# Four PSUM banks held for good in one tile, and an earlier start of two dense tiles

## The chip, the cores and the metric

The kernel runs on one core of one Trainium2 chip. The metric is device time in microseconds (us), the median of several executions. All runs used below were marked as fast ones, and each kernel's ratio is taken against runs of the kernel before on the same chip. Differences between two other kernels are of medians, some from different chips; the kernel before took 335.0 to 335.7 us on all of them.

## The reference

The reference computes an attention over eight batches of eight heads, 576 tokens and 64 values per head: a pooled attention on every fourth position plus a local one over a narrow band. The result becomes `x` with 4608 rows of 512, and goes through two dense layers. Cut to what matters here:

```python
def reference(q, k, v, moe_w_in, moe_w_out):
    attn_out = _attn_ref(q, k, v)                 # [8, 8, 576, 64]; pooled + banded
    x = attn_out.transpose(0, 2, 1, 3).reshape(4608, 512)
    h = x @ moe_w_in                              # 512 -> 2048
    g = h - np.tanh(h)
    return g @ moe_w_out                          # 2048 -> 512
```

## The kernel before

The kernel does not issue its instructions by hand. Each step is declared with its engine, an estimated cost, and the keys that it reads and writes; a list scheduler written in the kernel's own Python fixes one order of all steps, and the instructions are built in that order. The framework that builds the program then adds the semaphore waits, from the tiles that each instruction touches. So there are two systems of dependencies: the scheduler's keys decide the order, and the framework's tiles decide what waits for what.

The kernel uses eight banks of PSUM, where TensorE leaves its results. Four (`ps_ts`, `ps_ox`) serve attention throughout. The other four first serve the attention of batch 0 as two tiles of two banks, and then the dense layers as four tiles of one bank:

```python
ps_ts = fixed("ps_ts", [128, 2, 512], FP32, pool=psum)
ps_ox = fixed("ps_ox", [128, 2, 512], FP32, pool=psum)
ps_hy = []

early = ExitStack()
psum_e = early.enter_context(tc.tile_pool(name="psum_e", bufs=1, space=PSUM))
ps_ts1 = fixed("ps_ts1", [128, 2, 512], FP32, pool=psum_e)
ps_ox1 = fixed("ps_ox1", [128, 2, 512], FP32, pool=psum_e)

def dense_banks():
    early.close()
    pool = ctx.enter_context(tc.tile_pool(name="psum_d", bufs=1, space=PSUM))
    ps_hy.extend(fixed("ps_hy", [128, 512], FP32, 4, pool=pool))
```

One tile of the first dense layer is four matmuls (K chunks 0 to 3, one per pair of heads), a tanh on ScalarE and a subtract on VectorE, both reading the bank:

```python
def mm1(kb, fc):
    slot, us, g = hy[0] % 4, un[0] % 3, kb % 2
    # ... cut
    cut = 3 if kb == 0 and fc < 4 else 2
    old = ["ts1", "ox1"] if kb == 0 and fc < 4 else []

    def mm(part):
        if not ps_hy:
            dense_banks()
        for dc in range(cut) if part == 0 else range(cut, N_DC):
            T.matmul(ps_hy[slot], w_in_sb[:, dc, fc * 128:(fc + 1) * 128],   # L777
                     xT[dc][:, kb * 512:kb * 512 + 512],
                     start=(dc == 0), stop=(dc == N_DC - 1))
    # ... the two parts become two steps on PE, of keys ("hy", slot) and old
    op("ACT", 490, lambda: A.activation(                                     # L786
        out=u[us], in_=ps_hy[slot], func=AF.Tanh), ...)
    op("DVE", 620, lambda: V.tensor_tensor(                                  # L789
        out=gT[g][:, fc, :], in0=ps_hy[slot], in1=u[us], op=ALU.subtract), ...)
```

The second dense layer (`mm2`) adds up 16 matmuls (L832) into one bank, which ScalarE copies out (L843). The scheduler interleaves them: usually two to four matmuls of one layer, then of the other, on different banks. One "round" below is the work for one output tile: 32 matmuls, four tanh, four subtracts and one copy. There are 36 of them.

The softmax here doesn't subtract the row's maximum and nothing guards it: scores larger than these inputs give would overflow.

## Time and profile before

| | before |
|---|---|
| time, median (range) | 334.98 us (334.89 to 335.55) |
| profiled span | 333.9 us |
| mean granted TensorE clock | 1.000 |
| TensorE idle | 333.9 - 319.9 = 14.0 us (rather less: 43 of 2606 matmuls left no record) |
| last attention matmul, then dense work only | one round takes 6.9 us |

The prediction shows the busy shares, groups and timelines that the argument rests on. One more row of the page belongs with them, the granted clock: the span is cut into 40 slices, and each digit is the clock that TensorE was granted in that slice, in tenths (9 is 90% or more).

```profile
PEclk9999999999999999999999999999999999999999
```

The clock is full from end to end.

### The profile page before, as it was taken

The page shows a single profiled execution, that of the slowest core. Times are in us where ns is not written, and L with a number is a line of the kernel's source. Part 1 is how long each engine was busy: PE and PEld are TensorE (multiplying, and loading weights), DVE is VectorE, ACT ScalarE, POOL GpSimd, SP SyncE. Part 2 cuts the span into 40 slices and gives each one's busy share as a digit, 9 for nine tenths or more (in the row PEclk, how much of TensorE's full clock was granted, in tenths as well). Part 3 has the DMA queues.
Part 4 walks back from the last instruction along what each step waited for, and adds up shares of the span by engine and source line. Part 5 has one row for each costly group of instructions (what it writes and reads, how often), then busy time and mean ns, then how long its engine had stood idle before and what let it go on. Part 6 is the DMA issues. An engine that isn't in the chain of part 4 may idle for free.

```text
span 333.9 us, 6822 instructions
## 1 busy us (share of the span) xinstructions
PE 319.9 (96%) x2563; PEld 168.2 (50%) x2606; DVE 236.0 (71%) x386; ACT 209.6 (63%) x338; POOL 154.2 (46%) x183
## 2 busy tenths in 40 slices
PE   8778999999989999999999999999999999999996
PEld 5454555655554555554444444444444444444444
DVE  3697989789998898899687878787666443343300
ACT  1775877769948678668878786976654444444411
POOL 8673766248789477794929385652000000000000
PEclk9999999999999999999999999999999999999999
DMA  6999999999982779998999889843233000100012
GB/s 208 261 389 305 322 326 287 242 273 251 311 258 72 214 191 273 242 248 221 226 257 253 210 239 204 152 97 90 59 75 73 33 31 31 63 33 31 31 69 91
DMA packets 96878, 60.47 MB, mean 181 GB/s; under 512 B 74510, under 2 KB 80078, under 8 KB 96846
## 3 DMA queue, kind: packets, MB, share of 16 engines
q1 hardware_dynamic: 96846, 60.04, 67.2%
q8 instruction: 20, 0.33, 0.4%
q14 instruction: 12, 0.10, 0.1%
HBM read 43.05 MB, written 9.44 MB: 157 GB/s over the span
## 4 chain that ended last, share of the span: by engine, by line
PE 83%; DVE 9%; POOL 3%; issue 3%; ACT 1%; POOLq 0%; DVEq 0%; ACTq 0%
PE ps_hy L832 35%; PE ps_hy L777 34%; PE ps_ox L669 3%; PE ps_ts L587 3%; PE ps_ox L675 2%; DVE gT L789 2%; DVE ln L688 2%; PE ps_ts L520 2%; PE ps_hy L807 1%; DVE E L656 1%; DVE qk L529 1%; DVE half L533 1%; ACT qk L529 1%; DVE E L627 1%; PE ps_ox L606 1%
## 5 line engine op out<-in xcount | busy, mean ns | idle before, releaser
L777 PE MATMUL ps_hy<-xT,w_in_sb 128*128 128x512 bf16 x553 | 142.1, 379 | 2.3 <-issue 1.1
L832 PE MATMUL ps_hy<-w_out_sb,gT 128*128 128x512 bf16 x540 | 137.2, 379 | 1.4 <-issue 0.5
L789 DVE TENSOR_TENSOR gT<-ps_hy,uy 128x512 bf16<-128x512 f32 x144 | 95.1, 684 | 57.9 <-ACT uy L786 56.3
L786 ACT ACTIVATE uy<-ps_hy 128x512 f32<-128x512 f32 x144 | 83.6, 601 | 61.7 <-PE ps_hy L777 57.2
L777 PEld LDWEIGHTS <-w_in_sb 128*128 128x128 bf16 x576 | 53.1, 98 | 59.8 <-issue 1.7
L832 PEld LDWEIGHTS <-gT 128*128 128x128 bf16 x560 | 52.3, 98 | 58.1
L533 POOL TENSOR_TENSOR half<-qk 128x576 f32<-128x576 bf16 (+1 forms) x33 | 35.4, 1074 | 44.2 <-ACT qk L529 38.2
L688 DVE TENSOR_TENSOR ln<-ps_ox,r 128x896 bf16<-128x896 f32 x30 | 32.7, 1089 | 0.8
L623 ACT ACTIVATE E<-ps_ts 128x960 bf16<-128x960 f32 x30 | 29.4, 979 | 2.1 <-PE ps_ts L587 2.1
L843 ACT COPY uy<-ps_hy 128x512 f32<-128x512 f32 x35 | 20.6, 590 | 14.0 <-PE ps_hy L832 12.4
L443 POOL CAST vw<-vst 128x640 bf16<-128x640 f32 x27 | 23.6, 878 | 9.3 <-DMA vst<-in_v_dram 4.3
L627 DVE TENSOR_TENSOR E<-E,mask 128x960 bf16<-128x960 bf16 x28 | 24.4, 872 | 4.0 <-ACT E L623 3.8
L356 POOL TENSOR_TENSOR qkn<-qkn 128x512 f32<-128x512 f32 (+1 forms) x18 | 25.4, 1409 | 3.1 <-PE ps_ox L606 1.3
L529 ACT COPY qk<-ps_ts 128x1152 bf16<-128x1152 bf16 (+1 forms) x16 | 16.1, 1007 | 16.2 <-DVE qk L529 6.3
L708 DVE TENSOR_TENSOR xT<-lnT 128x480 bf16<-128x480 bf16 (+1 forms) x40 | 26.1, 668 | 0.0
L529 ACT COPY qk<-vst 128x1152 bf16<-128x1152 bf16 x10 | 22.1, 2207 | 1.2 <-POOL half L533 1.2
L538 POOL TENSOR_TENSOR qkd<-half 128x288 bf16<-128x288 f32 (+1 forms) x31 | 20.5, 664 | 5.0 <-DVE half L533 3.7
L491 DVE CAST qr<-qkn 128x1152 bf16<-128x1152 f32 (+1 forms) x18 | 17.8, 987 | 2.6 <-DMA qkn<-in_q_dram 2.2
L669 PEld LDWEIGHTS <-E 128*128 128x128 bf16 x300 | 15.2, 98 | 7.2 <-issue 0.8
L587 PEld LDWEIGHTS <-qk 64*128 64x128 bf16 x320 | 9.5, 95 | 17.8 <-issue 15.6
L669 PE MATMUL ps_ox<-vw,E 128*128 128x65 bf16 x300 | 18.0, 194 | 0.3 <-DVE xT L734 0.3
L491 POOL CAST qr<-qkn 128x1152 bf16<-128x1152 f32 (+1 forms) x14 | 15.8, 1129 | 5.1 <-DMA qkn<-in_k_dram 3.0
(107 smaller groups left out, 295.8 us busy)
## 6 DMA issues: line engine op xcount, KB each, us to landing
vst<-in_v_dram SPq DMA_DIRECT2D x62, 160.0 KB, 5.0
qkn<-in_q_dram SPq DMA_DIRECT2D x32, 288.0 KB, 4.2
qkn<-in_k_dram SPq DMA_DIRECT2D x32, 288.0 KB, 5.0
out_dram<-uy SPq DMA_DIRECT2D x35, 256.0 KB, 2.4
qkn<-in_v_dram SPq DMA_DIRECT2D x9, 512.0 KB, 5.1
gT<-in_moe_w_in_dram SPq DMA_DIRECT2D x4, 1024.0 KB, 8.8
xT<-in_moe_w_out_dram SPq DMA_DIRECT2D x8, 256.0 KB, 4.9
gT<-in_moe_w_out_dram SPq DMA_DIRECT2D x2, 1024.0 KB, 9.0
```

Source lines behind the costliest of these rows:

```text
L491: P.choice([(eng, ns, lambda fn=fn, x0=x0, x1=x1: fn(out=dst[:, x0:x1], in_=srt[:, x0:x1])) for eng, ns, fn in table], reads=[("qkn", sn, ...
L529: fn(out=o[:, ys].rearrange("p y (g a) -> p y g a", a=A6), in_=b16.rearrange("p (a g y) -> p y g a", a=A6, y=2)[:, ys])
L533: eng.tensor_tensor(out=half[:, ys], in0=four[:, ys, :, 0:2], in1=four[:, ys, :, 2:4], op=ALU.add)
L623: op("ACT", 980, lambda: A.activation(out=e1, in_=ps[:, :, 0:480], func=AF.Exp, scale=SCALE), reads=ts, writes=[("E", se, 0)], pri=URG.get ...
L627: op("DVE", 900, lambda: V.tensor_tensor(out=e1, in0=e1, in1=mask[:, 0:480].unsqueeze(1).to_broadcast([128, 2, 480]), op=ALU.mult), reads= ...
L669: T.matmul(po[:, hh, 65 * t:65 * t + 65], E[se][:, c:c + 128], vw[w][:, 2 * jj + hh, t, :], start=True, stop=True)
L688: op("DVE", 1090, lambda: V.tensor_tensor(out=ln[sl].rearrange("p n (h d) -> p h n d", d=D), in0=blocks[:, :, :, 0:64], in1=r[s].unsqueeze ...
L708: up=up: eng.tensor_tensor(out=xo[:, QW * t0:QW * t0 + nt * n].rearrange("p (t g a) -> p t g a", t=nt, a=4), in0=lnT[sl][:, t0:t0 + nt, 0: ...
L777: T.matmul(ps_hy[slot], w_in_sb[:, dc, fc * 128:(fc + 1) * 128], xT[dc][:, kb * 512:kb * 512 + 512], start=(dc == 0), stop=(dc == N_DC - 1))
L786: op("ACT", 490, lambda: A.activation(out=u[us], in_=ps_hy[slot], func=AF.Tanh), reads=[("hy", slot)], writes=[("u", us)], pri=-1)
L789: op("DVE", 620, lambda: V.tensor_tensor(out=gT[g][:, fc, :], in0=ps_hy[slot], in1=u[us], op=ALU.subtract), reads=[("hy", slot), ("u", us) ...
L832: T.matmul(ps_hy[slot], gT[g][:, fc, ts * 128:ts * 128 + 128], w_out_sb[:, fc, :], start=(fc == 0), stop=(fc == N_FF - 1))
```

## The change

The intent is to save the closing and opening of pools between batch 0 and the dense layers: the four banks become one tile for good, and both uses are slices of it. With the banks no longer tied to a pool that opens when all of batch 0's use is over, two dense tiles may begin on K chunks 0 and 1 in the two banks that pair 0 leaves first. Tables that say on which engine a copy or an addition goes, and how urgent a step is, were tuned anew.

```diff
-    ps_hy = []
-    early = ExitStack()
-    psum_e = early.enter_context(tc.tile_pool(name="psum_e", bufs=1, space=PSUM))
-    ps_ts1 = fixed("ps_ts1", [128, 2, 512], FP32, pool=psum_e)
-    ps_ox1 = fixed("ps_ox1", [128, 2, 512], FP32, pool=psum_e)
-
-    def dense_banks():
-        early.close()
-        pool = ctx.enter_context(tc.tile_pool(name="psum_d", bufs=1, space=PSUM))
-        ps_hy.extend(fixed("ps_hy", [128, 512], FP32, 4, pool=pool))
+    ps_e = fixed("ps_e", [128, 4, 512], FP32, pool=psum)
+    ps_ts1, ps_ox1 = ps_e[:, 0:2], ps_e[:, 2:4]
+    ps_hy = [ps_e[:, 2], ps_e[:, 3], ps_e[:, 0], ps_e[:, 1]]
 ...
-        cut = 3 if kb == 0 and fc < 4 else 2
-        old = ["ts1", "ox1"] if kb == 0 and fc < 4 else []
+        old, parts = [], (range(0, 2), range(2, 4))
+        if kb == 0 and fc < 4:
+            old = ["ox1"] if fc < 2 else ["ts1"]
+            parts = (range(0, 2), range(2, 3), range(3, 4)) if fc < 2 else (range(3), range(3, 4))
 ... (mm takes the list of chunks; one step on PE per part)
-    P_A, LATE = 5000, {0: 25, 2: 40, 3: 40}
+    P_A, LATE = 5000, {0: 40, 2: 40, 3: 40}
-    PV = {2: 0, 3: 0, 4: -1, 5: -1, 6: 0}
+    PV = {2: 0, 3: 1, 4: -1, 5: 0, 6: 1}
 ... (so too PLACE, CV, RE, TU, PV1, VD, RS, UP, TS, AS, URG and AD: entries of tables)
```

More of the change, by code (lines that the diff above doesn't have):

```diff
@@ L768, in mm1, with mm @@
         bs = sorted({kb * 512 // S, (kb * 512 + 511) // S})
-        cut = 3 if kb == 0 and fc < 4 else 2
-        old = ["ts1", "ox1"] if kb == 0 and fc < 4 else []
-        def mm(part):
-            if not ps_hy:
-                dense_banks()
-            for dc in range(cut) if part == 0 else range(cut, N_DC):
+        old, parts = [], (range(0, 2), range(2, 4))
+        if kb == 0 and fc < 4:
+            old = ["ox1"] if fc < 2 else ["ts1"]
+            parts = (range(0, 2), range(2, 3), range(3, 4)) if fc < 2 else (range(3), range(3, 4))
+        def mm(dcs):
+            for dc in dcs:
                 T.matmul(ps_hy[slot], w_in_sb[:, dc, fc * 128:(fc + 1) * 128],
@@ L779, in mm @@
                          start=(dc == 0), stop=(dc == N_DC - 1))
-        for part in range(2):
-            dcs = range(cut) if part == 0 else range(cut, N_DC)
-            op("PE", 216 * len(dcs), lambda part=part: mm(part),
+        for dcs in parts:
+            op("PE", 216 * len(dcs), lambda dcs=dcs: mm(dcs),
                reads=[("w_in", fc // 4, c) for c in dcs] +
                [(name, b, j) for b in bs for j in dcs for name in ("x", "xh")],
-               writes=[("hy", slot)] + old, pri=P_A if old and part == 0 else 5000)
+               writes=[("hy", slot)] + old, pri=P_A if old and dcs[-1] < 3 else 5000)
         op("ACT", 490, lambda: A.activation(
@@ L881 @@
     TB = {(1, 0), (1, 1), (2, 0), (2, 1), (3, 0), (5, 0)}
-    PV = {2: 0, 3: 0, 4: -1, 5: -1, 6: 0}
-    PLACE = {2: (1, 3), 3: (1, 2), 4: (4, 4), 5: (1, 2), 6: (4, 4), 7: (1, 1), 8: (3, 3)}
+    PV = {2: 0, 3: 1, 4: -1, 5: 0, 6: 1}
+    PLACE = {2: (0, 2), 3: (1, 2), 4: (4, 4), 5: (1, 2), 6: (4, 4), 7: (1, 1), 8: (3, 3)}
     W_LATE = [0, 0, 0, 0]
@@ L890 @@
               [("DVE", 500, V.tensor_copy)]]
-    CV = {0: 3, 1: 0, 2: 0, 3: 3, 4: 0, 5: 0, 6: 3, 7: 1, 8: 2, 9: 0, 10: 1, 11: 3}
+    CV = {0: 3, 1: 1, 2: 1, 3: 3, 4: 1, 5: 0, 6: 3, 7: 0, 8: 2, 9: 0, 10: 2, 11: 3}
     REORDER = [[("DVE", 860, V.tensor_copy), ("ACT", 950, A.copy),
@@ L895 @@
                [("DVE", 1150, V.tensor_copy)], [("POOL", 1350, GP.tensor_copy)]]
-    RE = {(0, 0): 0, (0, 1): 0, (1, 0): 1, (1, 1): 1, (2, 0): 1, (2, 1): 0, (3, 0): 3, (3,
-          1): 0, (4, 0): 2, (4, 1): 1, (5, 0): 0, (5, 1): 0}
+    RE = {(0, 0): 1, (0, 1): 4, (1, 0): 2, (1, 1): 4, (2, 0): 3, (2, 1): 4, (3, 0): 0, (3,
+          1): 0, (4, 0): 2, (4, 1): 4, (5, 0): 1, (5, 1): 1}
     TURN = [[("ACT", 1125, A.copy), ("DVE", 1250, V.tensor_copy)],
@@ L900 @@
             [("ACT", 2210, A.copy)]]
-    TU = {(0, 0): 0, (0, 1): 0, (1, 0): 2, (1, 1): 2, (2, 0): 0, (2, 1): 0, (3, 0): 2, (3,
-          1): 0, (4, 0): 0, (4, 1): 1, (5, 0): 1, (5, 1): 0}
+    TU = {(0, 0): 2, (0, 1): 1, (1, 0): 2, (1, 1): 1, (2, 0): 1, (2, 1): 1, (3, 0): 2, (3,
+          1): 1, (4, 0): 1, (4, 1): 1, (5, 0): 1, (5, 1): 1}
     re_v, re_a, re_p = (("DVE", 480, V.tensor_copy), ("ACT", 580, A.copy),
@@ L908 @@
               [("ACT", 600, A.copy)], [("DVE", 650, V.tensor_copy)]]
-    PV1 = True
-    VD = {0: 1, 1: 2, 2: 1, 3: 0, 4: 1, 5: 0, 6: 1}
-    RS = {(0, 1): 2, (1, 0): 4, (1, 1): 1}
-    UP = {0: 0, 1: 0, 2: 0, 3: 3, 4: 3, 8: 0, 11: 3}
+    PV1 = False
+    VD = {0: 2, 1: 0, 2: 1, 3: 1, 4: 1, 5: 0, 6: 1}
+    RS = {(0, 1): 2, (1, 0): 4, (1, 1): 3, (3, 0): 4}
+    UP = {0: 3, 1: 0, 2: 3, 3: 3, 4: 2, 6: 3, 8: 1, 11: 3}
     UP_COPY = [("ACT", 660, A.copy), ("DVE", 720, V.tensor_copy)]
@@ L920 @@
              [[half_p], [half_p]]]
-    TS = {(0, 0): 1, (0, 1): 2, (1, 1): 2, (2, 1): 2, (4, 0): 2, (5, 0): 2, (5, 1): 1}
-    AS = {(1, 0): 2, (1, 1): 1, (2, 0): 1, (2, 1): 1, (5, 0): 1, (5, 1): 4, (6, 1): 1}
-    URG = {'e1': {4: -2, 5: -2, 6: -2, 7: -2, 8: -2, 9: -2, 10: -2, 11: -2}, 'e2': {0: -2,
-          1: -2, 2: -2, 3: -2, 4: -2, 5: -2, 6: -2, 7: -2, 8: -2, 9: -2, 10: -2, 11: -2},
-          'norm': {0: -2, 1: -2, 2: -2, 3: -2, 4: -2, 5: -2, 6: -2, 7: -2}, 'add': {0: -2,
-          1: -2}, 'turn': {4: -2, 5: -2}, 'vd': {4: -2, 5: -2}}
+    TS = {(0, 0): 1, (0, 1): 2, (1, 1): 2, (2, 1): 2, (5, 0): 1, (5, 1): 3}
+    AS = {(0, 0): 1, (1, 0): 1, (1, 1): 1, (2, 0): 1, (4, 0): 1, (5, 0): 4, (5, 1): 4, (6,
+          1): 1}
+    URG = {'e1': {8: -2, 9: -2, 10: -2, 11: -2}, 'e2': {0: -2, 1: -2, 2: -2, 3: -2, 4: -2,
+          5: -2, 6: -2, 7: -2, 8: -2, 9: -2, 10: -2, 11: -2}, 'od': {0: -2, 1: -2}, 'norm':
+          {0: -2, 1: -2, 2: -2, 3: -2, 4: -2, 5: -2, 6: -2, 7: -2, 8: -2, 9: -2, 10: -2, 11:
+          -2}, 'add': {0: -2, 1: -2, 2: -2, 3: -2, 4: -2, 5: -2, 6: -2, 7: -2}, 'turn': {4:
+          -2, 5: -2}, 'vd': {2: -2, 3: -2}}
     ADDERS = [[("DVE", 760, 440, V), ("POOL", 1190, 850, GP)],
               [("POOL", 1190, 880, GP)], [("DVE", 760, 440, V)]]
-    AD = {(0, 0): 1, (0, 1): 0, (1, 0): 0, (1, 1): 1, (2, 0): 1, (2, 1): 0, (3, 0): 0, (3,
-          1): 1, (4, 0): 0, (4, 1): 0, (5, 0): 0, (5, 1): 2}
+    AD = {(0, 0): 2, (0, 1): 2, (1, 0): 0, (1, 1): 1, (2, 0): 0, (2, 1): 1, (3, 0): 0, (3,
+          1): 1, (4, 0): 0, (4, 1): 0, (5, 0): 2, (5, 1): 1}
     op("DVE", 180, lambda: V.memset(warm, 0.0), writes=["warm"], pri=-999)
```

## The prediction

> **What bounds the kernel now.** I read the page first: busy shares, then the group table, then the chain of waits.
>
> ```profile
> PE 319.9 (96%) x2563; PEld 168.2 (50%) x2606; DVE 236.0 (71%) x386; ACT 209.6 (63%) x338; POOL 154.2 (46%) x183
> PE 83%; DVE 9%; POOL 3%; issue 3%; ACT 1%; POOLq 0%; DVEq 0%; ACTq 0%
> L777 PE MATMUL ps_hy<-xT,w_in_sb 128*128 128x512 bf16 x553 | 142.1, 379 | 2.3 <-issue 1.1
> L832 PE MATMUL ps_hy<-w_out_sb,gT 128*128 128x512 bf16 x540 | 137.2, 379 | 1.4 <-issue 0.5
> L789 DVE TENSOR_TENSOR gT<-ps_hy,uy 128x512 bf16<-128x512 f32 x144 | 95.1, 684 | 57.9 <-ACT uy L786 56.3
> L786 ACT ACTIVATE uy<-ps_hy 128x512 f32<-128x512 f32 x144 | 83.6, 601 | 61.7 <-PE ps_hy L777 57.2
> L843 ACT COPY uy<-ps_hy 128x512 f32<-128x512 f32 x35 | 20.6, 590 | 14.0 <-PE ps_hy L832 12.4
> ```
>
> TensorE carries 83% of the chain, nearly all of it dense matmuls. Its idle column is tiny (2.3 and 1.4 us), while VectorE and ScalarE wait 58 and 62 us for each other and for it: they are followers. The timeline of a late stretch shows why TensorE does not wait for them:
>
> ```profile
> 259.04 1.03 PE L832 MATMUL ps_hy<-w_out_sb,gT 128*128 128x512 bf16 x4
> 259.24 0.60 ACT L786 ACTIVATE uy<-ps_hy 128x512 f32<-128x512 f32 x1 [1.07 <-PE ps_hy L777]
> 259.87 0.69 DVE L789 TENSOR_TENSOR gT<-ps_hy,uy 128x512 bf16<-128x512 f32 x1 [0.87 <-ACT uy L786]
> 259.90 1.03 PE L777 MATMUL ps_hy<-xT,w_in_sb 128*128 128x512 bf16 x4
> 260.77 1.89 PE L832 MATMUL ps_hy<-w_out_sb,gT 128*128 128x512 bf16 x8
> ```
>
> While ScalarE (259.24) and VectorE (259.87) read one finished bank, TensorE fills others. Four matmuls start every 0.86 us, 0.216 us each (eight take 1.89 = 7 x 0.216 + 0.379); a matmul's record of 0.379 is thus 0.216 of its own plus 0.163 of tail.
>
> The change aims at the timeline just before the dense layers:
>
> ```profile
> 28.66 0.81 PE L777 MATMUL ps_hy<-xT,w_in_sb 128*128 128x512 bf16 x2
> ...
> 28.85 0.40 ACT L734 CAST xT<-ps_ts 128x288 bf16<-128x288 f32 x1
> 29.29 0.46 DVE L734 CAST xT<-ps_ts 128x288 bf16<-128x288 f32 x1 [0.54 <-ACT xT L734]
> ...
> 29.80 1.46 PE L777 MATMUL ps_hy<-xT,w_in_sb 128*128 128x512 bf16 x6 [0.33 <-DVE xT L734]
> ```
>
> Dense work begins at 28.66 and then waits for the last K chunk. From 29.80 on, TensorE's waits of 0.2 us or more add up to about 1.3 us (0.30, 0.65 and 0.33 at 53, 94 and 101 us). Note also the two copies in the middle: the two halves of this copy lie in the two different banks of one tile, yet VectorE waited until ScalarE ended (29.25, plus 0.04). Waits in this program go by tile here, not by bank.
>
> **What the Trainium skill says.** "PSUM — Partial Sum Buffer", section "PSUM bank collisions raise a hardware error", says that two engines must not touch the same bank and quadrant at once, but pairs on different banks run clean. The trace agrees at 259 us: three engines at work on ps_hy, no wait. So four dense banks need no ordering among themselves. "TensorE: Matmul & The Clock Gate", section "Back-to-back issue gap", gives N/2.4 + 2.5 ns, 216 ns for 512 columns, as measured here. The same page's "A second HAM failure mode: psum-queue depth-cycling" tells of a kernel whose short idles between groups of matmuls made the clock oscillate; the kernel before never shows it (granted clock 1.00 in every stretch).
>
> **The change part by part.** (1) Two tiles may start on K chunks 0 and 1 early. In the built order only two matmuls move ahead of pair 3's last step, and four more follow it before the last chunk is needed: six done instead of three, so 3 x 0.216 = 0.65 us at best. (2) The tables move copies and adds among ScalarE, VectorE and GpSimd; what TensorE idles after 29.80 caps this at 1.3 us, plus perhaps a microsecond of start. The stated gain is therefore 1 to 3 us of 335, under 1%.
>
> (3) The dense banks were four tiles (ps_hy0 to ps_hy3); now they are slices of one tile, ps_e. I followed the waits of the built program to the instructions that raise the semaphores. In the program before, a tanh waits for its own bank's last matmul, and a bank's next matmul for its own subtract. In the changed one, every change of engine on ps_e is ordered against the access just before it, whichever bank that used: all 588 of 588 such changes, 575 of them between different banks. For instance the third K chunk of tile 1 waits for the tanh of tile 0; that tanh waits for tile 1's second chunk. So TensorE's dense matmuls, the tanh, the subtract and the output copies form one strict chain in which one engine works at a time.
>
> The chain after the first dense matmul has 255 runs of TensorE, 173 of ScalarE and 140 of VectorE. Its sum, from the rows above:
> - Until the first dense matmul, as before: 28.7.
> - TensorE: (576 + 560) x 0.216 = 245.4, and 3.5 for the 48 narrower matmuls of the last tile: 248.9.
> - ScalarE: 144 x 0.601 + 35 x 0.590 = 107.2, and three small copies, 1.0: 108.2.
> - VectorE: 144 x 0.684 = 98.5, and two small copies, 0.7: 99.2.
> - Handovers. From TensorE, 255 x (0.163 tail + 0.04) = 51.8. Into TensorE, 254 x 0.04 = 10.2; between the other two, 58 x 0.04 = 2.3. The 0.04 is what stood between ScalarE's end and VectorE's start at 29.25. In 165 handovers the wait stands on a separate wait instruction; the last two of these lines, from the end of the chain of waits, show 0.08 in place of 0.04:
>
> ```profile
> 327.40 3.55 PE ps_hy L807 x48
> 330.95 0.03 DVEq L815
> 330.99 0.04 issue
> 331.03 0.29 DVE uy L815
> ```
>
>   so 165 x 0.04 = 6.6 more. Together 70.9.
> - Attention matmuls. By their widths some 52 us follow the first dense one; by their place in the order about 34 stand where TensorE waits anyway, and 17.5 inside a run, where they lengthen the chain: 17.5.
> - The end: from 331.3 to 333.9, 2.6; and the timed figure is 1.1 above the profiled span (334.98 against 333.9).
>
> Sum: 28.7 + 248.9 + 108.2 + 99.2 + 70.9 + 17.5 + 2.6 + 1.1 = 577. To this I add what can only be guessed: in 139 places ScalarE or VectorE has attention work (241 us in all) between two steps of the chain. There is room for each in those gaps, but inputs that come late will hold up some tanh or subtract. At 0.12 us a place, my choice, that is 17 us: **594 us**.
>
> **Rivals.** *The chain does not bind, and the stated gain comes:* 332 to 335 us. For it: the hardware needs no such waits, and the copies on ScalarE and VectorE are short. Against it: the waits are in the program, and the halves at 29.29 show one holding an engine back across banks. I give it 2 to 3%. *The chain binds, but attention fills the holes better or worse:* this moves the 17.5 and the 17. If all attention matmuls fall into waits, 560; if each of the 139 places costs 0.5 us, 647. *The clock falls:* TensorE would be at work for about 300 of 594 us in pieces of 0.4 to 2 us with idles of 0.7 to 1.5. If such idles count as the cited section tells, dense matmuls could double in part of the run; a fifth of the run at half speed costs about 50 us more. The trace before has no stretch like it, so I give this one in six. *VectorE's subtract gets quicker when GpSimd is not beside it:* its range in the trace is only 630 to 692 ns, so at most 144 x 0.05 = 7 us less.
>
> **Range and chances.** The low end takes the sum with little interference and quicker subtracts, 560; the high end has interference of 0.5 us a place or a part at a lower clock, 660. Slower by over 2% has 0.97, from the waits being counted, not guessed; same 0.02; faster 0.01.
>
> **What would show it.** Right: TensorE busy near 300 us of some 590; the chain of waits alternating PE ps_e, ACT uy, PE ps_e, DVE gT, with ScalarE and VectorE about 18% each; TensorE's idle column naming ACT uy and DVE gT with 0.6 to 0.9 us each time. In the late stretch without attention one round of 32 matmuls, four tanh, four subtracts and one copy should take 6.9 + 2.4 + 2.7 + 0.6 + 8 x 0.203 + 9 x 0.04 = 14.6 us, where it takes 6.9 now. Wrong: TensorE still above 90% busy (waits satisfied early); or the granted clock below 1.00; or idles of TensorE named after attention work on ScalarE or VectorE, which would mean that my 17 us are too few.

## The result, and the profile after

| | before | after |
|---|---|---|
| time, median | 334.98 us | 655.37 us (653.56 to 656.87) |
| profiled span | 333.9 us | 652.7 us |
| mean granted clock | 1.000 | 0.832 |
| TensorE idle | 14.0 us | 652.7 - 435.4 = 217.3 us |
| first dense matmul | 28.66 us | 30.59 us |

The ratio is 1.955 (95% interval 1.949 to 1.962). Every ratio in this document is the mean time of one kernel's fast runs over that of the other's fast runs in the same rounds, so it is not quite the ratio of the medians quoted. The result is correct. The changed kernel is slower by 95%.

The page of the changed kernel: the busy shares, the granted clock, the shares of the chain of waits by engine, and the groups (busy us, mean ns of one, then idle time just before them and what ended most of it). Line 768 stands where 777 stood, 822 where 832 did, 779 for 789, 776 for 786 and 833 for 843. PEld is TensorE's weight load, POOL is GpSimd, SP is SyncE, a q after an engine's name stands for its sequencer, and "issue" for time in which the engine waited for nothing that the profile shows.

```profile
PE 435.4 (67%) x2602; PEld 190.3 (29%) x2602; DVE 225.1 (34%) x388; ACT 216.7 (33%) x341; POOL 144.9 (22%) x181
...
PEclk9976699797699999998789899777876785686659
...
PE 58%; DVE 18%; ACT 17%; issue 4%; DMA 1%; SPq 1%; DVEq 0%; ACTq 0%
...
L768 PE MATMUL ps_e<-xT,w_in_sb 128*128 128x512 bf16 x576 | 192.8, 455 | 98.1 <-DVE gT L779 64.4
L822 PE MATMUL ps_e<-w_out_sb,gT 128*128 128x512 bf16 x560 | 182.8, 440 | 105.0 <-ACT uy L776 52.1
L779 DVE TENSOR_TENSOR gT<-ps_e,uy 128x512 bf16<-128x512 f32 x144 | 99.0, 691 | 368.1 <-PE ps_e L822 155.8
L776 ACT ACTIVATE uy<-ps_e 128x512 f32<-128x512 f32 x144 | 85.3, 597 | 310.8 <-PE ps_e L822 163.5
```

Three things are to be seen. First, the idle columns of the two dense groups of TensorE went from 2.3 and 1.4 us to 98.1 and 105.0, and they name the subtract and the tanh. Second, the subtract and the tanh cost the same as before (691 and 597 ns), but wait longest for L822, the second layer's matmuls, whose results they never read. That is an ordering between banks, not a flow of data. Third, the clock row has digits below 9, most of them late, and the mean matmul record is 440 to 455 ns instead of 379.

The span grew by 318.8 us: TensorE's idle time by 203.3 and its busy time by 115.5. The view of waits of TensorE (us in total, times, longest) says whom it waited for:

```profile
PE ps_e L768 <- DVE gT L779: 64.4, 77, 1.6
PE ps_e L822 <- ACT uy L776: 52.1, 70, 1.5
PE ps_e L768 <- ACT uy L776: 30.6, 42, 1.8
PE ps_e L822 <- ACT uy L833: 26.9, 26, 2.9
```

The six rows for dense matmuls (two smaller ones are left out) add up to 203 us in 246 waits. That is about the whole growth of the idle time. In the first and second row, first-layer matmuls wait for a subtract and second-layer matmuls for a tanh, one engine handing to the next.

The timeline of a late stretch, where only dense work is left, shows single steps (start us, length us, engine, line, operation, idle before and its releaser):

```profile
521.04 0.59 PE L822 MATMUL ps_e<-w_out_sb,gT 128*128 128x512 bf16 x2 [0.74 <-ACT uy L776]
521.74 0.69 DVE L779 TENSOR_TENSOR gT<-ps_e,uy 128x512 bf16<-128x512 f32 x1 [5.77 <-PE ps_e L822]
522.48 0.59 PE L768 MATMUL ps_e<-xT,w_in_sb 128*128 128x512 bf16 x2 [0.85 <-DVE gT L779]
523.11 0.69 DVE L779 TENSOR_TENSOR gT<-ps_e,uy 128x512 bf16<-128x512 f32 x1 [0.68 <-PE ps_e L768]
...
532.37 3.33 PE L768 MATMUL ps_e<-xT,w_in_sb 128*128 128x512 bf16 x8
...
541.01 1.01 PE L768 MATMUL ps_e<-xT,w_in_sb 128*128 128x512 bf16 x2 [0.78 <-DVE gT L779]
541.82 1.06 PE L822 MATMUL ps_e<-w_out_sb,gT 128*128 128x512 bf16 x2
```

Read it downwards: the second, third and fourth line each begin 0.04 to 0.11 us after the one above ends. TensorE, VectorE, TensorE, VectorE: never two at once, where the kernel before had three engines at work at 259 us. The last three lines are the same kind of work at the lower clock: eight matmuls take 3.33 us, where the prediction shows eight in 1.89, and two take 541.82 - 541.01 = 0.81 us from start to start, 0.405 each, instead of 0.216. Between them, at 536.44 and 537.77 us, pairs again took 0.59 us as in the first line. So a granted clock between 0.5 and 1 is a mean here: stretches at the full rate and stretches at about half of it.

The windows view gives, for a stretch, its length, the busy time (and count) of PE, PEld, DVE, ACT and POOL, the granted clock, the DMA share and GB/s. The first two stretches are single rounds from output copy to output copy; the third is all that follows the last attention matmul.

```profile
516.00:531.05 15.05, 8.19 (x32) 3.08 (x32) 2.77 (x4) 2.97 (x5) 0.00 (x0) 1.00 0.05 17
531.05:551.57 20.52, 13.66 (x32) 4.23 (x32) 2.77 (x4) 2.97 (x5) 0.00 (x0) 0.60 0.03 13
455.40:652.70 197.30, 127.75 (x396) 44.48 (x393) 28.81 (x45) 30.33 (x52) 0.00 (x0) 0.71 0.06 20
```

The two rounds hold the same instructions. One has the full clock and takes 15.05 us; the other is granted 0.60 and takes 20.52. Rounds in this part took 15.05 to 20.65 us; the prediction had 14.6 and assumed the full clock. So there are two costs to keep apart: the chain, and a clock that falls.

### The profile page after: what moved, and what is told of

Same layout as the page of the kernel before. It is cut to its first block, busy times and chain, and to the rows that moved or that the text cites. A ratio compares the mean times of both kernels' runs of the same rounds, so it can differ in the third digit from the quotient of the medians.

```text
span 652.7 us, 6923 instructions
## 1 busy us (share of the span) xinstructions
PE 435.4 (67%) x2602; PEld 190.3 (29%) x2602; DVE 225.1 (34%) x388; ACT 216.7 (33%) x341; POOL 144.9 (22%) x181
## 4 chain that ended last, share of the span: by engine, by line
PE 58%; DVE 18%; ACT 17%; issue 4%; DMA 1%; SPq 1%; DVEq 0%; ACTq 0%
PE ps_e L768 28%; PE ps_e L822 26%; DVE gT L779 15%; ACT uy L776 13%; ACT uy L833 3%; DMA qkn<-in_k_dram 1%; DVE ln L679 1%; SPq L397 1%; PE ps_e L797 1%; PE ps_ox L660 1%; PE ps_ts L578 1%; PE ps_ts L511 0%; DMA vst<-in_v_dram 0%; PE ps_ox L666 0%; DVE qk L520 0%
## 5 line engine op out<-in xcount | busy, mean ns | idle before, releaser
L768 PE MATMUL ps_e<-xT,w_in_sb 128*128 128x512 bf16 x576 | 192.8, 455 | 98.1 <-DVE gT L779 64.4
L822 PE MATMUL ps_e<-w_out_sb,gT 128*128 128x512 bf16 x560 | 182.8, 440 | 105.0 <-ACT uy L776 52.1
L779 DVE TENSOR_TENSOR gT<-ps_e,uy 128x512 bf16<-128x512 f32 x144 | 99.0, 691 | 368.1 <-PE ps_e L822 155.8
L776 ACT ACTIVATE uy<-ps_e 128x512 f32<-128x512 f32 x144 | 85.3, 597 | 310.8 <-PE ps_e L822 163.5
L768 PEld LDWEIGHTS <-w_in_sb 128*128 128x128 bf16 x576 | 62.0, 109 | 199.0 <-issue 164.0
L822 PEld LDWEIGHTS <-gT 128*128 128x128 bf16 x560 | 59.3, 108 | 204.6 <-issue 172.8
L833 ACT COPY uy<-ps_e 128x512 f32<-128x512 f32 x35 | 20.5, 585 | 65.2 <-PE ps_e L822 28.4
L699 DVE TENSOR_TENSOR xT<-lnT 128x480 bf16<-128x480 bf16 (+1 forms) x40 | 20.9, 538 | 0.0
L666 PE MATMUL ps_ox<-vd,E 128*128 128x65 bf16 x232 | 17.8, 203 | 0.0
L511 PEld LDWEIGHTS <-qr 128*128 128x128 bf16 x198 | 14.7, 109 | 7.0 <-issue 4.2
```

The source lines that it names most:

```text
L699: up=up: eng.tensor_tensor(out=xo[:, QW * t0:QW * t0 + nt * n].rearrange("p (t g a) -> p t g a", t=nt, a=4), in0=lnT[sl][:, t0:t0 + nt, 0: ...
L776: op("ACT", 490, lambda: A.activation(out=u[us], in_=ps_hy[slot], func=AF.Tanh), reads=[("hy", slot)], writes=[("u", us)], pri=-1)
L779: op("DVE", 620, lambda: V.tensor_tensor(out=gT[g][:, fc, :], in0=ps_hy[slot], in1=u[us], op=ALU.subtract), reads=[("hy", slot), ("u", us) ...
L822: T.matmul(ps_hy[slot], gT[g][:, fc, ts * 128:ts * 128 + 128], w_out_sb[:, fc, :], start=(fc == 0), stop=(fc == N_FF - 1))
L833: op("ACT", 490, lambda: A.copy(out=y[ys], in_=ps_hy[slot]), reads=[("hy", slot)], writes=[("y", ys)], pri=-1)
```

## The experiments

The theory: one tile for four banks makes the framework order every access after the one before, whichever bank it used, and this costs all but a little; the low clock comes of TensorE's pauses and adds some tens of microseconds. The rivals: the new tables or the early start cause the loss; or the clock, not the chain, is most of it. All nine kernels below gave correct results.

### The changed kernel with its banks as tiles of their own

```diff
-    ps_e = fixed("ps_e", [128, 4, 512], FP32, pool=psum)
-    ps_ts1, ps_ox1 = ps_e[:, 0:2], ps_e[:, 2:4]
-    ps_hy = [ps_e[:, 2], ps_e[:, 3], ps_e[:, 0], ps_e[:, 1]]
+    early_t, early_x = ExitStack(), ExitStack()
+    ps_ts1 = fixed("ps_ts1", [128, 2, 512], FP32, pool=early_t.enter_context(
+        tc.tile_pool(name="psum_t", bufs=1, space=PSUM, side="right")))
+    ps_ox1 = fixed("ps_ox1", [128, 2, 512], FP32, pool=early_x.enter_context(
+        tc.tile_pool(name="psum_x", bufs=1, space=PSUM)))
+    ps_hy = []
+    def dense_banks(slot):
+        if slot < len(ps_hy):
+            return
+        n = len(ps_hy) // 2
+        (early_x, early_t)[n].close()
+        pool = ctx.enter_context(tc.tile_pool(name=f"psum_d{n}", bufs=1, space=PSUM,
+                                              side=("left", "right")[n]))
+        ps_hy.extend(fixed(f"ps_hy{n}", [128, 512], FP32, 2, pool=pool))
 ...
         def mm(dcs):
+            dense_banks(slot)
```

> The changed kernel with one part undone: the four dense banks are again four tiles of one bank each, with the early start and the new tables kept (the two banks that pair 0 leaves become free first, the other two after pair 2). Theory (the waits by tile are the whole loss): about 333.5 us, 332 to 335, TensorE over 95% busy, granted clock 1.00. Rival (the new tables or the early start upset the order of work): it stays well above 345 us.

Measured: 337.60 us (337.29 to 337.89) against 335.35 for the kernel before on the same chip, ratio 1.006 (1.004 to 1.008); clock 0.999. The early start and the new tables are still in it. The page's busy shares and its first dense group:

```profile
PE 323.0 (96%) x2602; PEld 167.8 (50%) x2602; DVE 233.8 (70%) x388; ACT 211.0 (63%) x341; POOL 153.0 (46%) x181
...
L782 PE MATMUL ps_hy<-xT,w_in_sb 128*128 128x512 bf16 x576 | 145.1, 379 | 0.3 <-DVE gT L793 0.2
```

TensorE is back at 96% with 0.3 us of idle before this group, and a matmul record is back at 379 ns. The order of instructions is that of the changed kernel on every engine; the two built programs were compared. So it is the tile that costs 655.4 - 337.6 = 318 us, not the tables or the early start. The expectation (332 to 335 us) missed by 2.6 us: the two other parts together bring no gain but a loss of 0.6%. That is looked into below.

### The kernel before, with nothing but the one tile

```diff
-    (ps_hy, psum_e, ps_ts1, ps_ox1 and dense_banks as above)
+    ps_e = fixed("ps_e", [128, 4, 512], FP32, pool=psum)
+    ps_ts1, ps_ox1 = ps_e[:, 0:2], ps_e[:, 2:4]
+    ps_hy = [ps_e[:, 2], ps_e[:, 3], ps_e[:, 0], ps_e[:, 1]]
 ...
-            if not ps_hy:
-                dense_banks()
```

> The kernel before with one part of the change alone: ps_hy0 to ps_hy3 and the four early banks become slices of one tile; order of start and tables as before. Theory: about 650 us (620 to 680), granted clock 0.80 to 0.87, since the chain of TensorE, ScalarE and VectorE comes with the one tile alone. Rival (tables or early start carry a part of the loss): clearly below 620 us.

Measured: 669.74 us (667.42 to 671.53), ratio 1.995 (1.989 to 2.002), clock 0.807. It lies in the range expected. Its chain of waits:

```profile
PE 58%; DVE 17%; ACT 17%; issue 5%; DMA 1%; SPq 1%; DVEq 0%; ACTq 0%; POOL 0%; POOLq 0%
```

The one tile alone, with the old order and tables, makes the whole loss, so the first rival falls from both sides. It is even 14 us slower than the changed kernel; its clock was also lower. At the rate found below (0.65 us for each us by which the clock is short), 0.193 x 666.2 - 0.168 x 652.7 = 19 us more of shortfall would make an estimated 12 of the 14.

### The changed kernel with two tiles of two banks

```diff
-    ps_e = fixed("ps_e", [128, 4, 512], FP32, pool=psum)
-    ps_ts1, ps_ox1 = ps_e[:, 0:2], ps_e[:, 2:4]
-    ps_hy = [ps_e[:, 2], ps_e[:, 3], ps_e[:, 0], ps_e[:, 1]]
+    ps_ts1 = fixed("ps_ts1", [128, 2, 512], FP32, pool=psum)
+    ps_ox1 = fixed("ps_ox1", [128, 2, 512], FP32, pool=psum)
+    ps_hy = [ps_ox1[:, 0], ps_ox1[:, 1], ps_ts1[:, 0], ps_ts1[:, 1]]
```

> The changed kernel with the four banks in two tiles of two banks each, in place of one tile of four; all else kept. Theory (one chain per tile): two chains that can overlap, each with half the dense work; about 420 us, 370 to 480, clearly between 335 and 655. Rival (a shared tile costs the same whatever its size, or the loss has another cause): within 5% of 655 us, or within 5% of 335 us.

Measured: 407.52 us (406.55 to 408.07), ratio 1.214 (1.210 to 1.218). The page's busy shares and chain:

```profile
PE 339.8 (84%) x2602; PEld 169.1 (42%) x2602; DVE 234.9 (58%) x388; ACT 213.4 (53%) x341; POOL 149.3 (37%) x181
...
PE 50%; DVE 18%; ACT 13%; issue 9%; POOL 4%; DMA 3%; SPq 2%; DVEq 0%; ACTq 0%; POOLq 0%
```

Two tiles of two banks cost 407.5 - 337.6 = 70 us, one tile of four 318. This is the dose that the theory asks for: with two tiles there should be two chains, and while one is with ScalarE or VectorE the other may be with TensorE. It brings something else: TensorE is idle for 16% of this run, and still the granted clock was 1.000. So this much idle time alone does not lower the clock.

### The changed kernel with TensorE kept busy in its waits

To measure the clock's share, five matmuls of 320 columns on a constant tile are put before each run of dense matmuls that follows another engine's access, in a bank of `ps_ts` that is free after the last attention pair (no bank is free before). Nothing reads them.

```diff
+    def fill():
+        if done[0] and turn_of[0] == "other":
+            for _ in range(5):
+                T.matmul(ps_ts[:, 0, 0:320], warm[:, 0:128], warm, start=True, stop=True)
+        turn_of[0] = "PE"
 ... (fill() ahead of the matmuls of mm1 and mm2; tanh, subtract and copy set turn_of to "other")
```

> The changed kernel with five dummy matmuls of 320 columns (0.67 us) put before each dense run of TensorE that waits for ScalarE or VectorE, only after the last attention pair (from about 455 us on), into a bank that attention no longer uses. They fall into waits of 0.8 us and add nothing to the chain. Theory (TensorE's idles lower its clock, which is the 60 us by which the sum was short): the granted clock in the last stretch rises from 0.69 to above 0.95, the stretch from 455 us to the end falls from 198 to about 155 us, and the whole to about 612 us (600 to 625). Rival (the low clock is not from idles): clock and time stay, or the dummies make it longer, 655 to 700 us.

Measured: 620.15 us (616.11 to 622.21), ratio 1.846 (1.838 to 1.855), clock 0.906. The windows of one round and of all that follows the last attention matmul, as shown for the changed kernel above:

```profile
508.32:523.37 15.05, 13.62 (x72) 6.98 (x72) 2.77 (x4) 2.97 (x6) 0.00 (x0) 1.00 0.05 19
459.40:619.50 160.10, 141.96 (x777) 73.78 (x774) 28.84 (x45) 30.33 (x52) 0.00 (x0) 1.00 0.07 25
```

With some 380 matmuls more (777 against 396) this stretch is 197.3 - 160.1 = 37.2 us shorter. Its clock is 1.00, not 0.71. Every round takes 15.05 us but for one of 14.83, exactly what the one full-clock round of the changed kernel took, so the fillers cost the chain nothing, and 15.05 is the chain's own cost. The time of the whole fell by 35.2 us.

This gives a rate. In the stretch the clock was short by 0.29 x 197.3 = 57 us, which cost 37.2: 0.65 us for each. The slow round was short by 0.40 x 20.52 = 8.2 and cost 20.52 - 15.05 = 5.5: 0.67. Over the whole changed kernel the clock was short by 0.168 x 652.7 = 110 us. At 0.65 that is an estimated 71 us of its time, of which 37 are shown and the rest is carried over from the same rate.

The changed kernel's trace gives a second estimate. Of its dense matmuls, 179 after 455.4 us took over 0.1 us more than 0.216 (or, at the end of a run, than 0.379), 36 us in all, which agrees with the 37.2 measured. Before it, 146 did, and lost 29. That makes 65 us, or 69 with the smaller excesses. So the second rival falls too: without the low clock the kernel would still take about 584 to 590 us.

### The 2 us that remain: the tables alone, and the early start alone

The first is the kernel before with the changed kernel's tables, no line else. The second has banks as tiles of their own and the early start, with the tables of before.

```diff
-    P_A, LATE = 5000, {0: 25, 2: 40, 3: 40}
+    P_A, LATE = 5000, {0: 40, 2: 40, 3: 40}
 ... (first kernel: all other tables of the change as well)
```

> The kernel before with the new tables alone; banks and start of the dense layers as before. Theory: within 1% of before, 333 to 337 us. Rival (the tables cost or gain much): outside that.

> The kernel before with the early start alone, each dense bank its own tile, tables as before. Theory: 334 to 336 us; at best 0.65 us of dense work comes forward. If the tables are what the early start needs, it may be up to 1 us slower than before.

Measured: tables alone 337.45 us (336.44 to 337.70), ratio 1.005 (1.003 to 1.007); early start alone 337.37 (336.90 to 337.73), ratio 1.006 (1.003 to 1.008). Each costs about 2 us, and both together also about 2 (337.60), so the losses do not add. Neither is the gain intended, and both expectations missed: 333 to 337 us for the tables, by 0.45, and 334 to 336 for the early start, by 1.4.

With the tables, dense work resumes on the last K chunk at 31.25 us instead of 29.80: pair 3 is ready 1.45 us later. The early start does what it should at first. TensorE's timeline in that kernel:

```profile
28.91 7.43 PE L782 MATMUL ps_hy<-xT,w_in_sb 128*128 128x512 bf16 x32
```

There is no wait at 29.80 any more; two matmuls had been done from 26.02 on and four more by 29.80, six instead of three, 3 x 0.216 = 0.65 us ahead. But the last copy on VectorE starts at 332.63 instead of 331.03, 1.6 us late. The scheduler makes one order for everything, and moving two steps on TensorE changed the order in dozens of places on TensorE, in 20 to 30 on VectorE and 13 to 23 on ScalarE (by how closely steps are told apart), and in 11 on GpSimd. The windows view over 71 to 110 us shows where most of it went, here for the early start:

```profile
71.00:110.00 39.00, 35.78 (x364) 19.80 (x362) 34.44 (x52) 29.40 (x52) 30.89 (x35) 1.00 0.80 220
```

and here for the kernel before:

```profile
71.00:110.00 39.00, 37.30 (x366) 20.59 (x370) 36.31 (x55) 30.51 (x53) 30.40 (x34) 1.00 0.81 221
```

TensorE is busy 1.5 us less in the same 39 us. Of the 0.65 + 1.6 = 2.25 us lost after the start, 1.5 lie here; the rest I did not place.

### The two pools alone

The kernel before with the two pools of the first experiment, opened at the moment where it opened its one pool, with no early start; the order of instructions is that of before.

```diff
-    (psum_e and dense_banks() as before)
+    (psum_t, psum_x and dense_banks(slot) of the first experiment)
 ...
-            if not ps_hy:
-                dense_banks()
+            for n in (0, 2):
+                dense_banks(n)
```

> The kernel before with its early banks only regrouped: two pools of two banks each, handed to the dense layers one after the other, so that an early start would be possible; no early start, every engine's order of instructions unchanged. Theory (the 2 us that the run with the early start lost come from the changed order of work after it): same as before, 335.0 to 335.6 us. Rival (the two pools cost the 2 us): about 337.4 us.

Measured: 335.55 us (335.49 to 336.86) against 335.22, ratio 1.0015 (0.9996 to 1.0033). No difference is resolved, so the arrangement in pools is not what the 2 us come from.

### The early start for one tile only

```diff
-            old = ["ox1"] if fc < 2 else ["ts1"]
-            parts = (range(0, 2), range(2, 3), range(3, 4)) if fc < 2 else (range(3), range(3, 4))
+            old = ["ox1"] if fc < 1 else ["ox1", "ts1"]
+            parts = (range(0, 2), range(2, 3), range(3, 4)) if fc < 1 else (range(3), range(3, 4))
```

The lines taken out are those of the kernel with the early start alone; its tables and pools stay. Against the kernel before, this keeps the order of every engine but for nine matmuls in three places.

> As the run with the early start alone, but only tile 0 begins early, so that the order of instructions differs from the kernel before in nine places of TensorE's queue and nowhere on the other engines. Theory: two matmuls fall into a wait before the dense layers and nothing later moves, so 0.3 to 0.7 us are gained: 334.6 to 335.1 us. Rival (an early start costs by itself, whatever the order): 336 to 337.5 us.

Measured: 335.75 us (334.88 to 336.72) against 335.22, ratio 1.0012 (0.9990 to 1.0033). The time lies between the ranges of the theory and of the rival; the expected gain did not show. TensorE's timeline says why:

```profile
25.76 0.59 PE L782 MATMUL ps_hy<-xT,w_in_sb 128*128 128x512 bf16 x2
...
29.80 1.46 PE L782 MATMUL ps_hy<-xT,w_in_sb 128*128 128x512 bf16 x6 [0.76 <-DVE xT L738]
```

Two matmuls went forward by three microseconds, and the next six still start at 29.80, after a wait of 0.76 us instead of 0.33. They wait for the copy of the last K chunk, which did not move. The same three dense matmuls lie before that wait as in the kernel before, only earlier.

### The kernel before with the last K chunk asked for later

The first three chunks of tile 1 go ahead of the last chunk of tile 0 on TensorE; nothing else moves.

```diff
     def emit(self, banks=None, end=None, filler=None):
         order = self.order()
+        order.remove(self.firsts[2])
+        order.insert(order.index(self.firsts[1]), self.firsts[2])
 ... (mm1 notes its steps' numbers in firsts)
```

> The kernel before with its own banks, tables and order, and one move in TensorE's queue: the first three K chunks of tile 1 stand ahead of the last chunk of tile 0, so that they fall into the wait for pair 3's last copy (29.3 to 29.8 us). No early start and no change of banks. Theory: what is left of the change's aim is 0.5 us, 334.7 us against 335.2, a ratio of 0.998 to 0.999; the lowest time of all these kernels. Rival (the wait moves on to the next stage): no difference, ratio 1.000 or above.

Measured: 335.80 us (334.45 to 335.88) against 335.66, ratio 0.9987 (0.9968 to 1.0007). The size is as expected, but it is not told apart from nothing. TensorE's timeline:

```profile
28.69 5.45 PE L780 MATMUL ps_hy<-xT,w_in_sb 128*128 128x512 bf16 x23
...
34.79 0.68 PE L523 MATMUL ps_ox<-ident,qr 128*128 128x128 bf16 x9 [0.65 <-DVE qr L494]
```

The wait at 29.80 is gone, and 5 us later TensorE waits 0.65 us for a reorder on VectorE, where the kernel before did not wait. That reorder ended at 34.73 us instead of 34.22: it started 0.14 us later, after subtracts that came later too (tile 0's last chunk, and so the first tanh, had moved back from 30.21 to 30.40), and took 1.42 us instead of 1.05. So the swap itself held up part of what follows; why the reorder took longer is not shown. No version that I ran clearly beats the kernel before.

## Why the prediction was right

The time on record was 594 us within 560 to 660; 655.4 lies in the range, 5 us below its upper end. The direction and the chain were right. That the range held is in part luck: the one tile with the old order and tables, much the same chain at a granted clock of 0.807, took 669.7 us and would have fallen outside. And one of the prediction's own signs of being wrong came, a granted clock below 1.00. Point by point:

- **The chain from the counted waits: right, and shown.** Taking the one tile away from the changed kernel removes the loss (337.6 us); putting it alone into the kernel before makes it (669.7); halving it gives a part (407.5). The named signs came: TensorE's idle names DVE gT and ACT uy, in the two largest rows 0.8 us (64.4/77) and 0.7 us (52.1/70) at a time, and the chain has VectorE at 18% and ScalarE at 17% where about 18% was said for each. One piece of the evidence was weaker than said: the halves of the copy at 29.29 also write into one tile outside PSUM (`xT`), so that line does not tell which tile ordered them. The counted waits do, and a second count in the built programs gave the same 588 and 575; in the kernel before, 31 of 611 such changes have that wait.
- **The round of 14.6 us: nearly right.** At the full clock it is 15.05, in the changed kernel and in the one with fillers. The handovers were a little dear: from 521.04 to 521.74 one pair of matmuls and its handover, with a wait instruction of its own, took 0.70 us, where the working gives 0.432 + 0.163 + 0.08 = 0.675 (its 0.08 stands in the second and third line of its view, from 330.95 to 331.03, not in the last two). The 0.216 us per matmul hold at the full clock. The section "Back-to-back issue gap" that the prediction names for it in the Trainium skill gives that figure for a single matmul and about 131 ns for a stream with weight loads; the stream here took 216 (eight in 1.89 us), so the measurement decides.
- **The clock: a rival at one in six and about 50 us, and it is what happened.** The granted clock fell to 0.832 over the run, and the cost is estimated at 65 to 71 us, 37 of them shown. This term should have been in the sum. The prediction saw the mechanism, but took the kernel before's full clock as evidence against it, though that kernel's TensorE is idle for 14.0 us in all.
- **The 17 us for attention work in the chain's way: they hardly came.** In the changed kernel's trace, the 567 gaps in which one engine hands `ps_e` to the next add up to 36.4 us, where the sum had 70.9 - 41.6 = 29.3 without the tails. Only five gaps are longer than 0.15 us, with under 2 us of waiting in them. So the guess of 17 was too large by about 15, and the handovers, 0.064 us each, too small by about 6. The 17.5 for attention matmuls inside a run holds: TensorE's runs on `ps_e` take 376.7 us, and 17 to 21 are left after 248.9, the tails' 41.6 and the clock's 65 to 69. With 1.9 us for the later start (30.59 against 28.66) the terms now add up to the miss: 65 to 69 + 1.9 + 6 - 15 makes 58 to 62, and the miss is 61. That the two largest errors have opposite signs kept it from being larger. The split leans on the count of slow matmuls; before 455 us no experiment stands behind that.
- **TensorE busy near 300 us: wrong, 435.4.** The 300 counted starts to starts at the full clock. In the chain every one of the 255 runs also shows its tail, 255 x 0.163 = 42 us, and matmuls at half rate are longer. Over before, busy time grew by 115.5; less these 42, there are 74 left, near the 65 to 71 that were estimated for the clock in other ways.
- **The stated gain of 1 to 3 us: wrong in sign.** Early start and tables cost 0.6% once the tile is out of the way. The 0.65 us of the early start are real in the trace (six matmuls done instead of three), but the step from there to the end failed: a new order on four engines came with it, and TensorE's idle time at 71 to 110 us grew by 1.5. That the new order is the cause is argued, from the two runs that kept the order or nearly so and lost nothing that could be resolved; it is not shown.

Two things stay open. What cannot be run without a free bank is the same filling before the last attention pair, so the clock's cost there, 29 us by the count and 34 by the rate, is only estimated. And which pattern of pauses lowers the clock is not settled: with two tiles it stayed at 1.000, with one it fell in some rounds and not in others that hold the same instructions.

## What to carry to other kernels

When several engines use PSUM banks in turn, give each bank a tile of its own, because the waits in this program went by tile; slices of one tile turned a pipeline into a chain here, at nearly twice the time. Follow the waits of the built program for a few instructions before believing that a layout change is free: two engines that wait for a result they never read are the sign. And doing work earlier in front of a fixed arrival can gain only if more is done before that arrival, and the next wait can take it back: the early start for two tiles, for one, and the swap gained nothing here that could be measured.

## What the Trainium skill lacked or had wrong

- No page says that waits may be inserted by tile and not by bank. "PSUM — Partial Sum Buffer", section "PSUM bank collisions raise a hardware error", gives bank and quadrant as the unit to guard. In the built program all 588 changes of engine on the one tile were ordered against the access just before, 575 of them between different banks, which cost 318 us of 655, the fall of the clock included (337.6 us with tiles of their own). That is a property of how the program was built, not of the chip, but a reader of the page alone would not look for it.
- "TensorE: Matmul & The Clock Gate", section "HAM oscillation — how this bites in real kernels", gives as the abstract rule that TensorE should not be idle for more than about 3.4 us. In the changed kernel the longest wait of TensorE was 2.9 us, after 455 us 1.5, and the granted clock was still only 0.832 and there 0.71; so keeping single pauses under that figure was not enough. The page's next section, the one below, allows for that.
- The same page's section on depth-cycling tells of short idles that make the clock oscillate, but it gives no pattern or size. Here, rounds with 32 x 0.216 = 6.9 us of matmuls in 15 to 21 us and pauses of about 0.7 to 1.5 us were granted 0.60 in one and 1.00 in another; TensorE busy for 84% kept 1.000; filling the pauses restored 1.00 and saved 37.2 us of 197.3.
